# An attention stage with two MLPs behind it: the linear part of the first MLP formed as (h w_in)ᵀ scaled by alpha times w_out

## The chip, the cores and the metric

The kernel runs on one core of a Trainium2 chip. The metric is the device time of one execution in microseconds, the median of several runs. Lines are named by their number in the kernel before (L585 is line 585).

## The reference

12480 tokens of 128 channels go through an attention over 32 inducing points and then through two MLPs with a hidden width of 2048.

```
scale = 1/sqrt(128)
def mab(q, kv):                       # a softmax, then a @ kv
    s = scale * (q @ kv.T);  s -= s.max(-1)
    a = exp(s);  a /= a.sum(-1) + 1e-9
    return a @ kv
h  = mab(inducing, x)                 # first attention: 32 x 128
x1 = mab(x, h)                        # second attention: 12480 x 128
t  = x1 @ w_in                        # 12480 x 2048
y1 = (max(t, 0) + alpha * min(t, 0)) @ w_out
y2 = max(y1 @ w2_in, 0)**2 @ w2_out   # the output, float32
```

The kernel uses two identities. With a the softmax weights of the second attention, x1 = a h, so t = a (h w_in) and the 32 x 2048 matrix h w_in can be made once. And max(t,0) + alpha min(t,0) = (1 - alpha) max(t,0) + alpha t, so that y1 = relu(t) ((1 - alpha) w_out) + a V with the small matrix V = h w_in diag(alpha) w_out. V is the linear part.

## The kernel before

Inputs come as 64-bit floats and are converted on the chip, piece by piece (512 columns each, four pieces for each of the four weights). `to_f32` (L179) makes four steps of a piece: `magnitude` and `low`, one pass each on ScalarE (ACT); `bits` on VectorE (DVE); `sign`, which is one DVE instruction and an addition on GpSimd (POOL) that writes the float32 piece. `conv_w_out` (L212) adds three: `rest` (POOL) multiplies the piece by 1 - alpha into `aw`; `split` rounds that to `wo_hi` (ACT) and puts the remainder into `wo_lo` (POOL); `scaled` overwrites `aw` with alpha times w_out, in four ACT instructions. `convs[0..3]` are the pieces of w_in, `convs[4..7]` those of w_out.

The first attention runs over seven groups of tokens (L353 to L408): scores, maxima, exponentials, transposes and values, with a running maximum. One piece is converted beside each group, up to `convs[4]`. The tail (L387 to L426) combines the groups and gives `hT`, the transposed h (L420). Ahead of and behind `hT` stand four calls of `transpose_w_in` (L379): four TensorE transposes and an ACT copy each, which give `wiT`.

From L526 on the second attention of the first token tile (`first`) and of tiles 1 to 3 (`second`) is prepared, and h w_in is made in four pieces: `make_w1s(k)` on TensorE, `split_w1s(k, 0)` on ACT and `split_w1s(k, 1)` on DVE. `first[6]` and `first[7]` spread the softmax weights over the partitions and write `a_s`, which the first hidden matmul (L585) reads.

The main loop (L738) is written out by hand as steps s = 0, 1, ...: at each, `l1_a(s)` makes one 128-wide slice of the hidden layer (matmul L585, Relu on ACT L589, remainder on DVE L591); `l1_b` (three matmuls) follows 3 to 5 steps later, the second MLP 24 steps later. One tile of tokens takes 16 steps. A `plan` adds further work to steps: the pieces of w_out that are left, `make_w1s(2)` at s=2 and `make_w1s(3)` at s=5, `second[2]` to `second[6]` at s=0 to 7, and the pieces of the second MLP's weights at s=11, 13, 17 and later. V is made by `step_u` (s=16 to 19, 16 matmuls of `wiT` with `aw`), `copy_u` and `step_v` (s=20); it is wanted at s=22.

Every engine works through its instructions in the order in which they are written, and so does the queue of SyncE (SP) that issues the DMAs. `second[6]` (s=7) issues 12 DMAs there, the load of the third weight piece of the second MLP (w2_out piece 0, `at(9, load_w, ...)`) stands right behind them, and ACT's `magnitude` of that piece is planned at s=17. PSUM banks go round: h1 and h2 have two each, which odd and even l1_a share with `make_w1s(0)` and `(1)`.

Of the kernel before, what the change touches and what calls it, by code (L numbers as in the profile page):

```python
# [25 lines left out]
Q = 4  # L26
# [3 lines left out]
def attention_then_two_mlps(ctx: ExitStack, tc, x, inducing, w_in, w_out, alpha, w2_in, w2_out, out):  # L30
# [7 lines left out]
    P = 128  # L38
# [61 lines left out]
    ident = cv.tile([P, P], F32, name="ident", tag="u_sb", bufs=1)  # L100
    make_identity(nc, ident)

    same = st_tile("same", [P, P])
# [25 lines left out]
    wiT = keep.tile([P, DFF], F32, name="wiT", tag="w2o_hi")  # L129
# [49 lines left out]
    def to_f32(name, k, place):  # L179

        v = {}

        def magnitude():
            raw = raws.pop((name, k))
            v["h"], v["l"] = raw[:, :, 1], raw[:, :, 0]
            v["m"] = cv.tile([P, 512], F32, name="mag", tag="mag", bufs=3)
            nc.scalar.mul(v["m"], v["h"].bitcast(F32), 2.0**-112)  # L190
# [12 lines left out]

        return [magnitude, low, bits, sign]
# [7 lines left out]
    def conv_w_out(k):  # L212
        chunks, cols = slice(4 * k, 4 * k + 4), slice(k * 512, (k + 1) * 512)
        f, hi, lo, a = (v.rearrange("p c d -> p (c d)")[:, cols] for v in (w_out_sb, wo_hi, wo_lo, aw))

        def rest():
            nc.gpsimd.tensor_tensor(
                aw[:, chunks], w_out_sb[:, chunks], al1[:, chunks].unsqueeze(2).to_broadcast([P, 4, P]), op=ALU.mult
            )

        def scaled():
            for c in range(4 * k, 4 * k + 4):
                nc.scalar.activation(aw[:, c, :], w_out_sb[:, c, :], AF.Copy, scale=al[:, c : c + 1])

        def split():
            nc.scalar.copy(hi, a)
            pool_lo(lo, a, hi)


        return to_f32("w_out", k, lambda: f) + [rest, split, scaled]  # L230
# [122 lines left out]
    for g in range(last):  # L353
# [13 lines left out]
        if g:  # L367
            convs[g - 1][3]()
# [10 lines left out]
    def transpose_w_in(k):  # L379
        b = y2_bank()  # L380
        for i in range(4):
            c = 4 * k + i
            nc.tensor.transpose(b[:, i * P : (i + 1) * P], w_in_sb[:, c * P : (c + 1) * P], ident)
        nc.scalar.copy(wiT[:, k * 512 : (k + 1) * 512], b)
# [18 lines left out]
    nc.vector.tensor_scalar_mul(nnm, nm[last], -1.0)  # L403
    wgt = att.tile([P, 1], F32, name="wgt", tag="wgt")
# [4 lines left out]
    run(convs[5][:2])  # L409
# [7 lines left out]
    transpose_w_in(0)  # L417
# [6 lines left out]
    transpose_w_in(1)  # L424
    run(convs[5][2:4])
    convs[4][4]()  # L426
# [98 lines left out]

    first = second_attention([0], [0, P, 2 * P])  # L526
# [25 lines left out]


    u_bank = []

    def step_u(k):
        if k == 0:
            u_bank.append(y2_bank())
        for c in range(4 * k, 4 * k + 4):
            nc.tensor.matmul(  # L560
                u_bank[0][:, :P], wiT[:, c * P : (c + 1) * P], aw[:, c, :], start=(c == 0), stop=(c == NCH - 1)
            )

    u_sb = cv.tile([P, P], F32, name="u_sb", tag="u_sb", bufs=1)

    def copy_u():
        nc.scalar.copy(u_sb, u_bank[0][:, :P])

    def step_v():
# [95 lines left out]
    AW = [8, 7, 16, 15]  # L665
# [117 lines left out]
```

## Time and profile before

| | us |
|---|---|
| median of 3 runs | 975.65 (975.25 to 976.1) |
| the profiled execution, whole | 976.26 |
| its span, first to last instruction | 974.2 |
| TensorE busy (matmul) | 960.8 |
| ACT / DVE / POOL busy | 756.2 / 671.9 / 543.8 |

The busy shares are means over a front part of some 95 us and a long main loop with other limits, so they are read by stretch. A line of the timeline gives the start, the duration, the engine, the source line, the output and the input, and in brackets how long the engine had been idle and what ended that.

### The profile page before, as it was taken

What the parts mean: (1) busy time and instruction counts of PE and PEld (TensorE: products, weight loads), DVE (VectorE), ACT (ScalarE), POOL (GpSimd) and SP (SyncE); (2) the same over time, 40 slices, a digit from 0 to 9 for tenths busy, and PEclk for the clock granted to TensorE, in tenths of its full rate; (3) what the DMA queues carried; (4) which work ended last, traced back from release to release, by engine and by line L of the source; (5) the groups of instructions that cost most, each with busy time, mean ns of one, the idle gap of its engine ahead of it and who ended that gap; (6) DMA issues with size and microseconds to landing.
All of it is one profiled execution on the core that took longest, in us unless ns stands there. A gap on an engine that the chain in (4) does not pass through costs nothing.

```text
span 974.2 us, 15128 instructions
## 1 busy us (share of the span) xinstructions
PE 960.8 (99%) x5034; PEld 882.3 (91%) x5034; DVE 671.9 (69%) x1130; ACT 756.2 (78%) x1501; POOL 543.8 (56%) x484
## 2 busy tenths in 40 slices
PE   9899999999999999999999999999999999999998
PEld 7677999998999989999899999899998999999997
DVE  6789776666766667666677666676666766666677
ACT  5689877777777777777787777787777777777776
POOL 2368765555665556655556555566555665555530
PEclk9989999999999999999999999999999999999999
DMA  9432002000020000110000200002000010000001
GB/s 329 152 92 68 9 3 46 11 10 1 10 48 10 1 10 10 28 21 10 10 10 3 46 11 10 1 11 48 10 1 10 10 32 18 10 10 10 1 10 19
DMA packets 65933, 28.35 MB, mean 29 GB/s; under 512 B 53968, under 2 KB 61760, under 8 KB 65856
## 3 DMA queue, kind: packets, MB, share of 16 engines
q1 hardware_dynamic: 64928, 27.29, 11.2%
q8 instruction: 39, 0.64, 0.3%
q14 instruction: 38, 0.31, 0.1%
q10 hardware_dynamic: 928, 0.11, 0.1%
HBM read 14.80 MB, written 6.39 MB: 22 GB/s over the span
## 4 chain that ended last, share of the span: by engine, by line
PE 95%; DVE 2%; ACT 2%; issue 1%; DMA 0%; ACTq 0%; DVEq 0%
PE y L595 18%; PE y L597 18%; PE y L596 18%; PE h L595 9%; PE h L597 9%; PE h L596 9%; PE h L585 9%; PE h L267 1%; PE ms L281 1%; PE y L331 1%; PE y L613 1%; PE ms L444 1%; DVE g1l L591 0%; DMA raw<-in_moe_w_out_dram 0%; ACT g1h L589 0%
## 5 line engine op out<-in xcount | busy, mean ns | idle before, releaser
L640 POOL TENSOR_TENSOR g2l<-sq,g2h 128x448 fp32r<-128x448 f32 (+1 forms) x424 | 486.6, 1148 | 343.7 <-ACT g2h L638 336.3
L591 DVE SCALAR_TENSOR_TENSOR g1l<-h,g1h 128x448 fp32r<-128x448 f32 (+1 forms) x448 | 277.6, 620 | 225.8 <-ACT g1h L589 220.5
L589 ACT ACTIVATE g1h<-h 128x448 fp32r<-128x448 f32 (+1 forms) x448 | 243.9, 545 | 136.0 <-PE h L585 132.3
L631 DVE TENSOR_TENSOR sq<-h,r 128x448 f32<-128x448 f32 (+1 forms) x448 | 278.4, 621 | 48.9 <-ACT r L629 4.8
L629 ACT ACTIVATE r<-h 128x448 f32<-128x448 f32 (+1 forms) x448 | 244.4, 545 | 54.3 <-PE h L597 8.8
L638 ACT CAST g2h<-sq 128x448 fp32r<-128x448 f32 (+1 forms) x448 | 249.4, 557 | 1.8 <-DVE sq L631 1.7
L585 PE MATMUL h<-a_s,w1s 128*128 128x448 f32 (+1 forms) x448 | 165.5, 371 | 3.2 <-DVE g1l L591 1.7
L595 PE MATMUL h<-y1h,w2i_hi 128*128 128x448 f32 (+1 forms) x448 | 162.7, 363 | 0.1
L597 PE MATMUL y<-g1l,wo_hi 128*128 128x448 f32 (+1 forms) x448 | 162.5, 363 | 0.0
L596 PE MATMUL y<-g1h,wo_lo 128*128 128x448 f32 (+1 forms) x448 | 162.4, 363 | 0.0
L595 PE MATMUL y<-g1h,wo_hi 128*128 128x448 f32 (+1 forms) x448 | 162.4, 362 | 0.0
L597 PE MATMUL h<-y1l,w2i_hi 128*128 128x448 f32 (+1 forms) x448 | 162.1, 362 | 0.2 <-DVE y1l L617 0.2
L595 PE MATMUL y<-g2h,w2o_hi 128*128 128x448 f32 (+1 forms) x448 | 162.1, 362 | 0.0
L597 PE MATMUL y<-g2l,w2o_hi 128*128 128x448 f32 (+1 forms) x448 | 162.1, 362 | 0.0
L596 PE MATMUL y<-g2h,w2o_lo 128*128 128x448 f32 (+1 forms) x448 | 162.0, 362 | 0.0
L596 PE MATMUL h<-y1h,w2i_lo 128*128 128x448 f32 (+1 forms) x448 | 161.9, 361 | 0.0
L585 PEld LDWEIGHTS h<-a_s,w1s 128*128 128x128 f32 (+1 forms) x448 | 84.9, 190 | 16.6 <-DVE g1l L591 5.7
L595 PEld LDWEIGHTS h<-y1h,w2i_hi 128*128 128x128 f32 x448 | 84.1, 188 | 7.3 <-DVE sq L631 1.4
L595 PEld LDWEIGHTS y<-g1h,wo_hi 128*128 128x128 f32 x448 | 84.5, 189 | 5.6 <-issue 0.5
L597 PEld LDWEIGHTS h<-y1l,w2i_hi 128*128 128x128 f32 x448 | 84.1, 188 | 5.9 <-DVE y1l L617 0.5
L597 PEld LDWEIGHTS y<-g2l,w2o_hi 128*128 128x128 f32 x448 | 84.1, 188 | 5.7 <-DVE g2l L640 0.2
L596 PEld LDWEIGHTS y<-g1h,wo_lo 128*128 128x128 f32 x448 | 84.4, 188 | 5.3
(127 smaller groups left out, 727.0 us busy)
## 6 DMA issues: line engine op xcount, KB each, us to landing
out_dram<-o SPq DMA_DIRECT2D x106, 56.0 KB, 1.9
xg<-in_x_dram SPq DMA_DIRECT2D x10, 512.0 KB, 8.8
raw<-in_moe_w_in_dram SPq DMA_DIRECT2D x8, 512.0 KB, 5.5
raw<-in_moe_w_out_dram SPq DMA_DIRECT2D x8, 512.0 KB, 4.9
a_s<-a_hi SPq DMA_DIRECT2D x54, 56.0 KB, 2.0
a_s<-a_lo SPq DMA_DIRECT2D x54, 56.0 KB, 1.9
xg<-in_x_dram SPq DMA_DIRECT2D x4, 256.0 KB, 3.5
out_dram<-o SPq DMA_DIRECT2D x4, 48.0 KB, 1.8
```

What stands on the lines that cost most here:

```text
L267: nc.tensor.transpose(b[:, k * p : (k + 1) * p], x_t[g][:p, i, k, :], ident[:p, :p])
L281: nc.tensor.matmul(b[i * M : (i + 1) * M, :n], indT, xT[:, t0 : t0 + n], start=True, stop=True, tile_position=(0, i * M),)
L585: nc.tensor.matmul(b[:, :w], w1s[: a.shape[0], c * P : (c + 1) * P], a, start=True, stop=True)
L589: nc.scalar.activation(hi, b[:, :w], AF.Relu)
L591: nc.vector.scalar_tensor_tensor(lo, b[:, :w], 0.0, f32(hi), op0=ALU.max, op1=ALU.subtract)
L595: nc.tensor.matmul(b, w_hi, hi, start=start, stop=False)
L596: nc.tensor.matmul(b, w_lo, hi, start=False, stop=False)
L597: nc.tensor.matmul(b, w_hi, lo, start=False, stop=stop)
L629: nc.scalar.activation(r, b, AF.Relu)
L631: nc.vector.tensor_tensor(sq, b, r, op=ALU.mult)
L638: nc.scalar.copy(hi, sq)
L640: (nc.vector if i >= total - LAG2 else nc.gpsimd).tensor_tensor(lo, sq, f32(hi), op=ALU.subtract)
```

## The change

The transposes of w_in, the sixteen `scaled` activations and `step_u` go. `step_wa` makes (h w_in)ᵀ, chunk by chunk of 128 hidden rows, from `w_in_sb` as the stationary operand and 32 columns of `hT`: eight chunks behind `make_w1s(0)`, four at s=0, four at s=1. `scale_wa` multiplies all of it by alpha in one DVE instruction (s=2). `step_v` multiplies it with `w_out_sb` (16 matmuls in four column groups, s=10); `copy_v` and `split_v` sum the four groups by a matmul with `same` (s=11, 14).

The conversions of w_out move: `convs[4]`'s `rest` and high part, and steps of `convs[5]`, `[6]` and `[7]`, stand in the tail of the first attention; `sign` and its POOL addition are now separate steps, and so are the high and the low part. `make_w1s(1)` and its `split` move from ahead of the loop to s=0, `second[2]` from s=0 to 1, `second[4]` from 2 to 3, `second[5]` from 4 to 5.

```diff
-    same = st_tile("same", [P, P])
+    same = keep_tile("same", [P, P])
...
+        def add():
+            nc.gpsimd.tensor_tensor(place().bitcast(I32), v["c"], v["l"], op=ALU.add)
+        return [magnitude, low, bits, sign, add]
...
-        def scaled():
-            for c in range(4 * k, 4 * k + 4):
-                nc.scalar.activation(aw[:, c, :], w_out_sb[:, c, :], AF.Copy, scale=al[:, c : c + 1])
-        def split():
+        def high():
             nc.scalar.copy(hi, a)
+        def low():
             pool_lo(lo, a, hi)
...
+    MAG, LOW, BITS, SIGN, ADD, REST, HI, LO = range(8)
     b = scores(last)
     values1(last - 1)
+    convs[4][REST]()
+    convs[5][MAG]()
+    convs[6][MAG]()
     maxima(last, b)
     exps(last, b)
     b = y2_bank()
     nc.tensor.transpose(b[:1, :P], nm[last], ident)
+    convs[4][HI]()
     transpose_e(last)
...
     nc.vector.tensor_scalar_mul(nnm, nm[last], -1.0)
+    convs[5][BITS]()
+    convs[5][SIGN]()
+    convs[6][BITS]()
...
     values1(last)
-    run(convs[5][:2])
+    convs[5][LOW]()
+    convs[5][ADD]()
+    convs[6][LOW]()
+    run(convs[7][:2])
...
-    transpose_w_in(0)
...                                   # here hT is made
-    transpose_w_in(1)
-    run(convs[5][2:4])
-    convs[4][4]()
+    convs[4][LO]()
+    convs[7][BITS]()
...
     first[0]()
     make_w1s(0)
-    transpose_w_in(2)
-    run(convs[6][:2])
+    step_wa(range(8))
     run(first[1:4])
     split_w1s(0, 0)
+    stage1.close()
+    run(first[4:6])
+    split_w1s(0, 1)
+    convs[6][SIGN]()
+    convs[6][ADD]()
+    convs[5][REST]()
+    convs[5][HI]()
+    first[6]()
     second[0]()
-    transpose_w_in(3)
-    stage1.close()
-    make_w1s(1)
-    convs[5][4]()
-    run(first[4:6])
-    convs[4][5]()
-    split_w1s(0, 1)
-    first[6]()
-    convs[6][2]()
     first[7]()
-    convs[6][3]()
-    convs[6][4]()
+    convs[7][SIGN]()
+    convs[6][REST]()
+    convs[5][LO]()
     second[1]()
-    split_w1s(1, 0)
...
-    at(0, convs[5][5])
+    at(0, step_wa, range(8, 12))
+    at(0, make_w1s, 1)
+    at(0, split_w1s, 1, 0)
+    at(0, convs[6][HI])
     at(1, split_w1s, 1, 1)
-    at(0, second[2])
+    at(1, step_wa, range(12, 16))
+    at(1, convs[7][ADD])
+    at(1, convs[6][LO])
+    at(1, second[2])
+    at(2, scale_wa)
     at(2, make_w1s, 2)
     at(2, split_w1s, 2, 0)
     at(2, second[3])
-    at(2, second[4])
-    at(3, convs[6][5])
-    at(5, split_w1s, 2, 1)
-    at(4, second[5])
-    at(2, convs[7][0])
-    at(5, convs[7][1])
-    at(5, convs[7][2])
+    at(3, convs[7][REST])
+    at(3, second[4])
+    at(4, split_w1s, 2, 1)
+    at(5, second[5])
     at(5, make_w1s, 3)
     at(5, split_w1s, 3, 0)
+    at(5, convs[7][HI])
+    at(5, convs[7][LO])
     at(7, split_w1s, 3, 1)
     at(7, second[6])
-    at(7, convs[7][3])
-    at(8, convs[7][4])
-    at(13, convs[7][5])
-    for k in range(4):
-        at(AW[k], convs[4 + k][6])
-        at(16 + k, step_u, k)
-    at(19, copy_u)
-    at(20, step_v)
+    at(10, step_v)
+    at(11, copy_v)
+    at(14, split_v)
```

The new functions:

```
def step_wa(chunks):                  # one PSUM bank for all chunks
    for c in chunks:
        matmul(wa_bank[:, c*M:(c+1)*M], w_in_sb[:, c*P:(c+1)*P], hT[:, :M])
def scale_wa():
    nc.vector.tensor_tensor(wa, wa_bank, al, op=mult)    # alpha broadcast over 32
def step_v():
    for c in range(NCH):
        q = c % Q
        matmul(v_bank[q*M:(q+1)*M, :P], wa[:, c, :], w_out_sb[:, c, :], tile_position=(0, q*M))
def split_v():
    matmul(bv[:, :P], same, v_sb)     # then v_s as before, on ACT and DVE
```

## Rows read from the trace of the kernel before

**Rows 1.** Windows view: stretch, length, busy us (count) of PE, PEld, DVE, ACT, POOL; clock, DMA share, GB/s

```profile
47.70:58.20 10.50, 9.25 (x22) 6.28 (x23) 9.82 (x18) 7.24 (x16) 6.10 (x5) 0.54 0.00 0
58.20:71.20 13.00, 12.57 (x78) 11.51 (x77) 10.21 (x17) 12.37 (x34) 7.43 (x6) 1.00 0.45 121
...
95.00:950.00 855.00, 855.00 (x4297) 796.98 (x4290) 580.76 (x947) 669.03 (x1309) 497.39 (x436) 1.00 0.07 14
```

**Rows 2.** Timeline, 35 to 48 us: first attention's tail to the first hidden matmul

```profile
35.16 0.69 ACT L306 ACTIVATE e<-ms,nm 128x512 f32<-128x512 f32 x1 [1.89 <-DVE nm L299]
...
37.62 0.29 DVE L407 TENSOR_SCALAR sel<-same,wgt 128x128 f32<-128x128 f32 x1 [1.17 <-ACT wgt L405]
...
39.83 0.42 DVE L197 TENSOR_SCALAR mag<-mag 128x512 int32<-128x512 int32 x1
...
40.28 0.69 DVE L201 SCALAR_TENSOR_TENSOR mag<-raw,mag 128x512 int32<-128x512 int32 x1
...
40.89 0.30 DVE L452 STREAM_TRANSPOSE a<-y 96x128 f32<-96x128 f32 x1
...
41.55 1.00 DVE L458 TENSOR_TENSOR a<-a,mx 96x128 f32<-96x128 f32 x1
...
43.64 0.29 ACT L461 ACTIVATE a<-a 96x128 f32<-96x128 f32 x1
...
45.37 0.69 DVE L522 TENSOR_TENSOR w1s<-h,w1s 64x512 fp32r<-64x512 f32 x1
...
46.09 0.94 DVE L197 TENSOR_SCALAR mag<-mag 128x512 int32<-128x512 int32 x1
46.37 0.47 ACT L505 CAST a_s<-y 96x384 fp32r<-96x384 f32 x1 [0.96 <-PE y L498]
...
47.06 0.55 DVE L507 TENSOR_TENSOR a_s<-y,a_s 32x384 fp32r<-32x384 f32 x1
...
47.67 1.33 PE L585 MATMUL h<-a_s,w1s 96*128 96x384 f32 x3 [1.34 <-DVE a_s L507]
```

**Rows 3.** Timeline, 41 to 47 us: one piece's steps on POOL and ACT

```profile
41.11 1.29 POOL L202 TENSOR_TENSOR w_out_sb<-mag,raw 128x512 int32<-128x512 int32 x1 [6.38 <-ACT wiT L384]
...
42.35 2.09 POOL L217 TENSOR_TENSOR aw<-w_out_sb,al 128x512 f32<-128x512 f32 x2
...
44.78 0.62 ACT L226 CAST wo_hi<-aw 128x512 fp32r<-128x512 f32 x1
...
45.48 1.27 POOL L207 TENSOR_TENSOR wo_lo<-aw,wo_hi 128x512 fp32r<-128x512 f32 x1 [1.04 <-ACT wo_hi L226]
```

**Rows 4.** Timeline, 48 to 59 us: terms of the loop's first eight steps

```profile
48.79 1.91 PE L517 MATMUL y<-w_in_sb,hT 128*128 128x512 f32 x2
...
50.03 1.27 DVE L458 TENSOR_TENSOR a<-a,mx 96x448 f32<-96x448 f32 x1
...
52.99 0.60 DVE L466 TENSOR_REDUCE sm<-a 96x14 f32<-96x448 f32 x1
...
53.99 0.95 DVE L591 SCALAR_TENSOR_TENSOR g1l<-h,g1h 128x384 fp32r<-128x384 f32 x2
...
55.19 0.64 DVE L474 STREAM_TRANSPOSE a2t<-a 96x448 f32<-96x448 f32 x1 [0.24 <-POOL a L470]
...
58.17 0.56 ACT L483 CAST a_hi<-a2t 96x448 fp32r<-96x448 f32 x1
```

**Rows 5.** Timeline, 58 to 72 us: alpha's activations, the SP queue, the late load

```profile
58.63 1.28 ACT L223 ACTIVATE aw<-w_out_sb,al 128x128 f32<-128x128 f32 x4
...
59.98 0.51 SPq L489 DMA_DIRECT2D a_s<-a_lo  x1
...
65.24 1.03 PEld L560 LDWEIGHTS y<-aw,wiT 128*128 128x128 f32 x8
...
66.92 0.53 SPq L172 DMA_DIRECT2D raw<-in_moe_w_out_dram  x1
...
71.23 0.68 ACT L190 ACTIVATE mag<-raw 128x512 f32<-128x512 f32 x1 [0.66 <-DMA raw<-in_moe_w_out_dram]
```

More of the change, by code (lines that the diff above doesn't have):

```diff
@@ L128, in attention_then_two_mlps @@
     w_out_sb = keep.tile([P, NCH, P], F32, name="w_out_sb", tag="w2i_lo")
-    wiT = keep.tile([P, DFF], F32, name="wiT", tag="w2o_hi")
     aw = keep.tile([P, NCH, P], F32, name="aw", tag="w2o_lo")
@@ L219, in rest @@
             )
-        def scaled():
-            for c in range(4 * k, 4 * k + 4):
-                nc.scalar.activation(aw[:, c, :], w_out_sb[:, c, :], AF.Copy, scale=al[:, c : c + 1])
-        def split():
+        def high():
             nc.scalar.copy(hi, a)
+        def low():
             pool_lo(lo, a, hi)
-        return to_f32("w_out", k, lambda: f) + [rest, split, scaled]
+        return to_f32("w_out", k, lambda: f) + [rest, high, low]
     def conv_w2(name, k, hi, lo):
@@ L367, in attention_then_two_mlps @@
         if g:
-            convs[g - 1][3]()
+            run(convs[g - 1][3:5])
         if 1 < g and g + 3 <= last:
@@ L377, in attention_then_two_mlps @@
             nc.vector.tensor_scalar(al1, al, -1.0, 1.0, op0=ALU.mult, op1=ALU.add)
[L379 to L384, printed above, removed]
+    MAG, LOW, BITS, SIGN, ADD, REST, HI, LO = range(8)
     b = scores(last)
     values1(last - 1)
+    convs[4][REST]()
+    convs[5][MAG]()
+    convs[6][MAG]()
     maxima(last, b)
@@ L524, in split_w1s @@
             nc.scalar.copy(dst, b)
+    wa = att.tile([P, NCH, M], F32, name="wa", tag="wa")
+    wa_bank = []
+    def step_wa(chunks):
+        if not wa_bank:
+            wa_bank.append(y2_bank())
+        for c in chunks:
+            nc.tensor.matmul(
+                wa_bank[0][:, c * M : (c + 1) * M], w_in_sb[:, c * P : (c + 1) * P], hT[:, :M], start=True, stop=True
+            )
+    def scale_wa():
+        nc.vector.tensor_tensor(
+            wa, wa_bank[0].rearrange("p (c j) -> p c j", j=M), al.unsqueeze(2).to_broadcast([P, NCH, M]), op=ALU.mult
+        )
     first = second_attention([0], [0, P, 2 * P])
@@ L529, in attention_then_two_mlps, with step_v, copy_v @@
     make_w1s(0)
-    transpose_w_in(2)
-    run(convs[6][:2])
+    step_wa(range(8))
     run(first[1:4])
     split_w1s(0, 0)
-    second[0]()
-    transpose_w_in(3)
-    stage1.close()
-    make_w1s(1)
-    convs[5][4]()
-    run(first[4:6])
-    convs[4][5]()
-    split_w1s(0, 1)
-    first[6]()
-    convs[6][2]()
+    stage1.close()
[6 more added lines that the diff above has]
+    first[6]()
+    second[0]()
     first[7]()
-    convs[6][3]()
-    convs[6][4]()
+    convs[7][SIGN]()
+    convs[6][REST]()
+    convs[5][LO]()
     second[1]()
-    split_w1s(1, 0)
     load_w("w2_in", 0)
     load_w("w2_in", 1)
[L554 to L559, printed above, removed]
+    v_bank = []
+    def step_v():
+        v_bank.append(y2_bank())
+        for c in range(NCH):
+            q = c % Q
             nc.tensor.matmul(
-                u_bank[0][:, :P], wiT[:, c * P : (c + 1) * P], aw[:, c, :], start=(c == 0), stop=(c == NCH - 1)
-            )
[L564 to L569, printed above, removed]
+                v_bank[0][q * M : (q + 1) * M, :P], wa[:, c, :], w_out_sb[:, c, :],
+                start=(c < Q), stop=(c >= NCH - Q), tile_position=(0, q * M),
+            )
+    v_sb = cv.tile([P, P], F32, name="v_sb", tag="v_sb", bufs=1)
+    def copy_v():
+        nc.scalar.copy(v_sb, v_bank[0][:, :P])
+    def split_v():
         bv = free_bank()
-        nc.tensor.matmul(bv[:, :P], hT, u_sb, start=True, stop=True)
+        nc.tensor.matmul(bv[:, :P], same, v_sb, start=True, stop=True)
         nc.scalar.copy(v_s, bv[:, :P])
@@ L664, in attention_then_two_mlps @@
     LAG1, LAG1_EARLY, LAG2, LAG2B, EARLY = 3, 5, 24, 4, 20
-    AW = [8, 7, 16, 15]
     PIECES = [
```

6 lines of the change are left out of this document (2 added, 4 removed).

## The prediction

> **What bounds the kernel now.** I read the windows view first. From 95 to 950 us TensorE's matmuls cover 855.00 of 855.00 us at full clock, 4297 of them, 0.199 us each [rows 1]. Nothing that the change touches lies there, so the time of the whole follows the front part one to one: if the loop reaches its saturated stretch 1 us later, the kernel ends 1 us later. The question is only when that is. In the front part two stretches matter. From 47.7 to 58.2 us TensorE ran at a granted clock of 0.54, so nearly all the time at its lower level of 1.2 GHz, and DVE was busy 9.82 of 10.50 us. From 58.2 to 71.2 us the clock was full and ACT was busy 12.37 of 13.00 us [rows 1]; ACT is the engine that the change relieves, so the eye goes there.
>
> Then I read the timeline of that ACT stretch, and how it ends. The piece of w2_out that ACT opens at s=17 begins at 71.23 us, and what ended ACT's idle time ahead of it (0.66 us) is a DMA [rows 5]. That DMA is issued at 66.92 us, because it stands in SP's queue behind the 12 issues of `second[6]`: the second of these is at 59.98 us, and eleven steps of 0.63 us lead to 66.92; it lands 4.3 us later [rows 5]. The 12 issues in turn start when ACT writes `a_hi` at 58.17 us [rows 4]. So a fixed 13.06 us lies between `a_hi` (s=7) and the opening of that piece (s=17), however little ACT has to do in between. I call it the lid. What counts is when `a_hi` comes.
>
> Last I read the timeline of the tail of the first attention, from 35 us to the first hidden matmul L585 at 47.67 us [rows 2], for what each moved step stands ahead of.
>
> **The change part by part, the stretch of ACT's relief.** Sixteen alpha activations leave ACT, four groups of 1.28 us, 5.1 us [rows 5]. They all stood between `a_hi` and s=17. Without them, and with the last high part (0.62 us [rows 3]) gone to s=5, ACT would have 13.06 - 0.66 - 5.1 - 0.62 = 6.7 us to do there. DVE has ten remainders of 0.48 us [rows 4], one split of 0.69 and two pieces' bits and signs at 0.42 and 0.69 [rows 2], with POOL's blocks about 9 us. Both lie under the lid, so the relief is worth only the 0.66 us of slack that it makes larger: nothing at the end. The matmuls for V go the same way: 32 loads of 0.129 us [rows 5] for u leave s=16 to 19, 32 loads for `step_wa` come in, and `step_v` at s=10, which the trace does not show, costs between 0 and those 4.1 us; it lies under the lid too, so 0 at the end. Behind s=17 ACT loses the copy of u and that of v, and DVE the remainder of v. Each has 128 columns; at the rate of the 384-wide pair, 0.95 us for 768 [rows 4], two are 0.3 us. The bounds are 0 and 0.95; I take -0.3.
>
> **The front part up to hT.** The two `magnitude` passes put ahead of the last exponential fall into ACT's wait of 1.89 us for the maximum [rows 2]: two of about 0.69 are 1.4. `rest` of piece 4 is a POOL step of 1.05 us (half of 2.09 [rows 3]) while POOL is free. Its high part, 0.62 us, goes between the last exponential and the copy of its transposes; bits, sign and bits on DVE, 0.42 + 0.69 + 0.42 = 1.53 us, go into DVE's idle 1.17 us before `sel` [rows 2], and the 0.4 us that sticks out is covered by the values matmuls, which `sel`'s reader comes behind. Were that cover gone, `hT` would be 0.4 us later. I take 0.
>
> **From hT to the first hidden matmul.** Here one thing gains and one loses. ACT no longer has a copy of `wiT` and the two passes of `convs[6]` ahead of the exponential L461, which stood at 43.64 us although its input was ready at 42.55 (41.55 + 1.00) [rows 2]. The input itself: `convs[7]`'s bits stand on DVE ahead of the transposes L452, where those of `convs[5]` stood at 39.83. At that time POOL is busy with `wo_lo` of piece 4: the addition of piece 5 can start when ACT's low pass is done, 37.6 + 0.7 = 38.3, takes 1.29, and `wo_lo` follows for 1.27, to 40.85 [rows 3]. The trace shows what such a bits step costs beside POOL: at 46.09 it took 0.94 us instead of 0.42 and ended 0.28 us after POOL's `wo_lo` had (45.48 + 1.27 = 46.75) [rows 2, 3]. So it ends at 41.1 us, or at 40.25 if POOL doesn't hold it. I take the first, as the row is of the same two instructions. (The Trainium skill, page "SBUF — State Buffer", section "Who interferes with whom", says the same more generally: the two engines share one pair of ports, and whichever comes second waits for the whole instruction of the other. By that the term is the first of the two, and the sum below +1.7; otherwise it would be +1.15.) L452 then starts at 41.15, the subtraction 0.66 later as before; it took 1.00 under POOL's addition, and between 0.15 and that without, I take 0.30, as the transpose of the same shape. The exponential starts at 42.15 us: 1.5 us sooner than before.
>
> From the exponential's start to DVE's `split_w1s(0, 1)` it took 1.73 us (43.64 to 45.37), so that one is at 43.9. And now the new wait. ACT's high part of piece 5 is written ahead of the copy of `a_s` in `first[7]`. It reads what POOL's `rest` of piece 5 writes, POOL has the addition of piece 6 ahead of that, and this addition waits for DVE's sign of piece 6, which stands behind the split. In a row: split to 44.6 (0.72 to the next start), sign 0.69 to 45.3, addition 1.29 to 46.6, `rest` 1.05 to 47.7, high part 0.62 to 48.3 [rows 2, 3]. Behind it are queued, on ACT, the copy of `a_s` (0.47), on DVE its remainder (0.55), and on TensorE the first L585: 49.4 us [rows 2]. Without the high part in front the copy could go when the spread is done, about 3.3 us sooner. The first L585 is thus at 49.4 against 47.67, **+1.7 us**, and TensorE has nothing to do for some 3.6 us before it.
>
> **From the first hidden matmul to a_hi.** Before: 47.67 to 58.17, 10.5 us. After, L585 of s=1 no longer follows directly. TensorE first has eight loads of `step_wa` and `make_w1s(1)`. At full clock that is 8 x 0.129 and about 0.9 us; at the lower level 8 x 0.26 and 1.75 to 1.91 us [rows 4, 5]. Which level? Before, it was the lower one through this whole stretch [rows 1], though TensorE had idled only 1.34 us directly ahead of it [rows 2]. After a longer hole I take the lower. [...] So L585 of s=1 starts 0.35 + 2.1 + 1.75 = 4.2 us after the first. ACT then does a split and the high part of piece 6 (two starts, 1.1 us) before its Relu of s=1 (0.5): 5.8 us. From there DVE has in order: remainder 0.5, split 0.72, maximum 0.60 (as the sum), subtraction 0.6 to 1.27, remainder 0.5, `scale_wa` 0.72 (not in the trace; between the 0.30 of a small transpose and the 1.27 of that subtraction; 512 PSUM columns like the split), remainder 0.5, sum with reciprocal 1.0 (52.99 to 53.99), remainder 0.5, split 0.72, remainder 0.5, transposes 0.64 [rows 2, 4]: 7.5 us. POOL's product lies beside them. `a_hi` comes 13.3 us after the first L585: **+2.8 us**; with the full clock 11.3 us, +0.8.
>
> **The sum.** +1.7 + 2.8 = +4.5 for `a_hi`; the lid passes it on to s=17; -0.3 behind that: +4.2 us. It is made in the profiled execution, whose 976.26 us (span 974.2) stand 0.6 us over the median; a difference carries over. 975.65 + 4.2 = 979.85 us.
>
> **The rivals.** *The clock stays up, or POOL doesn't hold the bits.* At full clock the sum is 1.7 + 0.8 - 0.3 = +2.2, without the hold another 0.55 less: 977.3 to 977.9 us; the hold gone and the clock low: 979.3. For it: `step_wa`'s 16 loads behind `make_w1s(0)` keep TensorE busy some 2 us longer. Against it: the 3.6 us hole.
>
> *A second drop of the clock.* ACT would idle some 4 us under the lid, and TensorE runs out of free banks with it. If the clock falls there, about four steps of s=18 to 22 run four matmuls at 0.4 instead of 0.2 us, 1.6 us against about 1.2 of ACT: +1.5, 981.3 us. In this stretch before TensorE was busy 12.57 of 13.00 us and the clock was 1.00 [rows 1], so nothing shows it.
>
> *Not slower: the wait in front of `a_s` is hidden.* That needs the high part of piece 5 to be done when the spread ends, near 44.8 us, so DVE's sign of piece 6 to be done by 41.8 us, 3.5 us sooner than I have it. Then the first L585 comes at 46.0, the hole is short, the clock full: -1.7 + 0.8 - 0.3 = -1.2, 974.45 us.
>
> *The lid doesn't hold.* If that load came earlier (issues faster than 0.63 us apart, or landed in less than 4.3 us), ACT's relief would count: the stretch would be DVE's 9 us instead of 13.06, -4. With the low clock +0.2, 975.85 us; with the full clock -1.8, 973.85 us. Against it: twelve issues in a row held that pace.
>
> **How the numbers follow.** Forecast 0.42; clock up or no hold 0.20; second drop 0.12; wait hidden 0.12; no lid 0.14. A measurement of this kernel tells about 0.2% (1.95 us) from no change, so the limits are 973.7 and 977.6 us. Slower: 0.42 + 0.12 + 0.12 of the first rival = 0.66. Same: the other 0.08, 0.08 of the hidden wait, 0.06 of no lid = 0.22. Faster: 0.04 + 0.08 = 0.12. The range leaves out the hidden wait and the better end of no lid: 975.5 to 982.0 us; the forecast's own range is 978.7 to 980.8.
>
> **What would show it.** The exponential L461 near 42 us; the high part of piece 5 ending near 48.3 with the copy of `a_s` right behind it and idle on its engine put down to POOL; the first hidden matmul near 49.4; `a_hi` near 62.7 after a stretch at the lower clock; ACT's wait for the DMA of w2_out grown from 0.66 to about 4 us; then the same course as before, later. If the copy of `a_s` starts with the spread's end, or if ACT's wait at s=17 has not grown, the prediction is wrong in that step.

## The result, and the profile after

The changed kernel takes 986.27 us, the median of four runs (985.43 to 989.03), against 975.67 us (975.25 to 976.1) before: a ratio of 1.0114 [1.0093, 1.0135]. That is 10.6 us slower where 4.2 were forecast, and outside the range. The profiled execution took 989.03 us with a span of 986.3, so it stands 2.8 us over its median; the two spans differ by 12.1 us.

The start of some rows in both profiled executions gives the places. The columns are the two durations, their difference, and the difference that the prediction had. hT is the end of DVE's L420 (after: L421); the first hidden matmul is L585 (after: L599); g(18) is ACT's Relu of s=18, r(28) and r(471) are ACT's first passes of the second MLP for s=28 and for the last step.

| stretch | before | after | differs | predicted |
|---|---|---|---|---|
| start to hT | 39.91 | 41.10 | +1.19 | 0 |
| hT to the first hidden matmul | 7.76 | 9.29 | +1.53 | +1.7 |
| to a_hi | 10.50 | 13.52 | +3.02 | +2.8 |
| to g(18) | 13.64 | 13.48 | -0.16 | 0 |
| to r(28) | 14.63 | 15.81 | +1.18 | -0.3 |
| to r(471) | 879.87 | 885.24 | **+5.37** | 0 |

The first line is not put down to the change: in this execution TensorE waited 1.12 us, up to 7.96 us, for a transfer of x, and in the other profiled executions hT comes between 39.5 and 40.9 us, in kernels with the changed front (39.5 to 40.9) as in those with that of before (39.8 to 40.2). The next four sum to +5.57 us, the last alone to +5.37.

The page of the kernel after, its span and the busy time of each engine:

```profile
span 986.3 us, 15141 instructions
...
PE 968.7 (98%) x5050; PEld 884.7 (90%) x5050; DVE 672.2 (68%) x1131; ACT 749.6 (76%) x1481; POOL 544.5 (55%) x484
```

ACT lost 6.6 us of work against the table of before, as the change meant, and TensorE's busy time grew by 7.9. The windows view of the front part, cut at hT, the first hidden matmul, a_hi and s=17 (columns: stretch, length, then busy time and instructions of PE, PEld, DVE, ACT and POOL, TensorE's granted clock, DMA share, GB/s):

```profile
41.10:50.40 9.30, 6.01 (x37) 3.51 (x37) 5.15 (x13) 1.77 (x4) 4.85 (x5) 0.74 0.16 56
50.40:63.90 13.50, 13.02 (x45) 9.92 (x46) 9.54 (x18) 6.55 (x14) 6.26 (x6) 0.68 0.01 1
63.90:76.80 12.90, 11.62 (x86) 9.56 (x84) 9.98 (x18) 7.76 (x18) 4.36 (x5) 1.00 0.42 118
76.80:91.40 14.60, 12.17 (x44) 9.95 (x44) 12.11 (x20) 12.90 (x27) 7.92 (x7) 0.77 0.48 160
```

The second line answers to the stretch at 0.54 in [rows 1]: 13.50 us instead of 10.50. The granted clock was at its lower level, 1.2 GHz, from 45.5 to 59.2 us (before: 47.2 to 57.5), and again from 79.6 to 86.5 us, which is the 0.77 of the fourth line; before had no such second drop. (An early one, from 8.0 to 11.4 us, belongs to the first line of the table.) The timeline shows the wait ahead of the first hidden matmul, and the late load:

```profile
40.71 1.28 POOL L208 TENSOR_TENSOR wo_lo<-aw,wo_hi 128x512 fp32r<-128x512 f32 x1
41.01 1.26 DVE L196 TENSOR_SCALAR mag<-mag 128x512 int32<-128x512 int32 x1
...
43.16 0.31 ACT L461 ACTIVATE a<-a 96x128 f32<-96x128 f32 x1 [2.11 <-DVE a L458]
...
46.44 1.28 POOL L203 TENSOR_TENSOR w_out_sb<-mag,raw 128x512 int32<-128x512 int32 x1 [4.45 <-issue]
47.68 2.04 POOL L218 TENSOR_TENSOR aw<-w_out_sb,al 128x512 f32<-128x512 f32 x2
48.76 0.62 ACT L223 CAST wo_hi<-aw 128x512 fp32r<-128x512 f32 x1 [4.82 <-POOL aw L218]
49.28 0.47 ACT L505 CAST a_s<-y 96x384 fp32r<-96x384 f32 x1
49.78 0.55 DVE L507 TENSOR_TENSOR a_s<-y,a_s 32x384 fp32r<-32x384 f32 x1 [3.48 <-ACT a_s L505]
50.39 0.69 PE L599 MATMUL h<-a_s,w1s 96*128 96x384 f32 x1 [2.57 <-DVE a_s L507]
...
63.91 0.57 ACT L483 CAST a_hi<-a2t 96x448 fp32r<-96x448 f32 x1 [0.98 <-DVE a2t L474]
...
76.82 0.67 ACT L189 ACTIVATE mag<-raw 128x512 f32<-128x512 f32 x1 [2.79 <-DMA raw<-in_moe_w_out_dram]
```

ACT stands 4.82 us in front of the high part of piece 5, waiting for POOL, and the copy of `a_s`, its remainder and the first hidden matmul follow in a row, as the prediction has it. At the lower end ACT now waits 2.79 us for the DMA of w2_out ([rows 5]: 0.66).

The other half is in the stretch that [rows 1] shows as covered in full. The windows view of 300 to 800 us, same columns, first of before, then of after:

```profile
300.00:800.00 500.00, 500.00 (x2511) 465.25 (x2510) 338.86 (x552) 390.19 (x763) 291.16 (x255) 1.00 0.07 14
```

```profile
300.00:800.00 500.00, 500.00 (x2495) 462.92 (x2495) 337.38 (x549) 387.72 (x757) 288.45 (x253) 1.00 0.07 13
```

TensorE is busy 500.00 us of 500.00 at full clock in both, but it gets 2495 matmuls done instead of 2511: 0.64% fewer, 3.2 us in these 500. Which ones, the groups of the same stretch tell (columns: line, operation, tiles, shape, count, busy us, mean ns of one, idle). Before, all ten forms have a mean of 362 to 364 ns, for instance:

```profile
L597 PE MATMUL y<-g2l,w2o_hi 128*128 128x448 f32 x246 | 89.2, 362 | 0.0
L596 PE MATMUL y<-g2h,w2o_lo 128*128 128x448 f32 x246 | 89.2, 362 | 0.0
```

After:

```profile
L610 PE MATMUL y<-g2h,w2o_lo 128*128 128x448 f32 x245 | 89.9, 367 | 0.0
L611 PE MATMUL y<-g1l,wo_hi 128*128 128x448 f32 x245 | 89.8, 367 | 0.0
L611 PE MATMUL y<-g2l,w2o_hi 128*128 128x448 f32 x245 | 89.6, 366 | 0.0
L609 PE MATMUL y<-g2h,w2o_hi 128*128 128x448 f32 x245 | 89.6, 366 | 0.0
...
L609 PE MATMUL y<-g1h,wo_hi 128*128 128x448 f32 x244 | 88.4, 362 | 0.0
L610 PE MATMUL h<-y1h,w2i_lo 128*128 128x448 f32 x244 | 88.4, 362 | 0.0
```

Four of the ten are longer by 3 to 5 ns: the three that use w2_out's halves and the one just ahead of them (consecutive matmuls overlap, so that a duration is longer than the pitch; from start to start it is 203.2 instead of 200.0 ns at these four places). These are the four pairs of neighbours of which one at least reads `w2o_hi`. Four times 3.2 ns in each of the 425 steps from s=46 to 471 is 5.4 us; the starts of the ACT passes put 5.3 us on them. The instructions there are the same in both kernels. What differs is where `w2o_hi` lies: in the program's allocation of SBUF it starts at byte 107424 of a partition before, in the place that it shares by its tag with `wiT`, and at 117440 after, since the change removes `wiT` and the tile is then made last. Each of the six other large weight tiles of the loop (`w1s`, `wo_hi`, `wo_lo`, `w2i_hi`, `w2i_lo`, `w2o_lo`) starts at a byte whose rest modulo 512 is 416 in both kernels (that of the small `v_s` is 32 in both); that of `w2o_hi` was 416 and is 192.

### The profile page after: what moved, and what is told of

It reads as the page before. It is cut to its first block, busy times and chain, and to the rows that moved or that the text cites. A ratio compares the mean times of both kernels' runs of the same rounds, so it can differ in the third digit from the quotient of the medians.

```text
span 986.3 us, 15141 instructions
## 1 busy us (share of the span) xinstructions
PE 968.7 (98%) x5050; PEld 884.7 (90%) x5050; DVE 672.2 (68%) x1131; ACT 749.6 (76%) x1481; POOL 544.5 (55%) x484
## 4 chain that ended last, share of the span: by engine, by line
PE 93%; DMA 2%; DVE 1%; ACT 1%; SPq 1%; issue 1%; POOL 0%; ACTq 0%; DVEq 0%
PE y L611 18%; PE y L610 18%; PE y L609 18%; PE h L609 9%; PE h L611 9%; PE h L610 9%; PE h L599 9%; DMA raw<-in_moe_w_in_dram 1%; DMA xg<-in_x_dram 1%; SPq L489 1%; PE y L627 1%; PE ms L444 1%; DMA raw<-in_moe_w_out_dram 0%; PE h L265 0%; PE ms L279 0%
## 5 line engine op out<-in xcount | busy, mean ns | idle before, releaser
L599 PE MATMUL h<-a_s,w1s 128*128 128x448 f32 (+1 forms) x448 | 167.2, 374 | 6.5 <-DVE g1l L605 3.2
L599 PEld LDWEIGHTS h<-a_s,w1s 128*128 128x128 f32 (+1 forms) x448 | 85.7, 191 | 22.9 <-DVE g1l L605 6.5
L610 PEld LDWEIGHTS y<-g2h,w2o_lo 128*128 128x128 f32 x448 | 84.6, 189 | 6.7
L611 PEld LDWEIGHTS y<-g1l,wo_hi 128*128 128x128 f32 x448 | 84.5, 189 | 5.5
```

Source lines behind the costliest of these rows:

```text
L599: nc.tensor.matmul(b[:, :w], w1s[: a.shape[0], c * P : (c + 1) * P], a, start=True, stop=True)
L610: nc.tensor.matmul(b, w_lo, hi, start=False, stop=False)
L611: nc.tensor.matmul(b, w_hi, lo, start=False, stop=stop)
```

## The experiments

Four theories: the address of `w2o_hi` costs 5 us in the loop; the high part of piece 5 ahead of the copy of `a_s` costs 3 to 4; the late load (the lid) and the second drop cost 1 to 2 together; and, as a rival to the first, something else that the change does slows the long loop (more traffic, another order). The median of before was 976.44 us beside e1 to e4, 976.77 beside e5 and e7 to e9, and 976.02 beside e6, e10 and e11. Since it moves by 1.1 us from 975.67 to the highest of these, each kernel is told by its difference from the before beside it, as after is by its 10.6 us; what one difference is less than another is called a gain.

**The changed kernel with `w2o_hi` where it was.** In e1 the tile is made at the point where `wiT` was, and starts at 107936 (rest 416):

```diff
+    w2o_first = keep.tile([P, DFF], F32R, name="w2o_hi", tag="w2o_hi")
     aw = keep.tile([P, NCH, P], F32, name="aw", tag="w2o_lo")
...
-            w2.extend(keep.tile([P, DFF], F32R, name=v, tag=v) for v in ("w2o_hi", "w2o_lo"))
+            w2.extend([w2o_first, keep.tile([P, DFF], F32R, name="w2o_lo", tag="w2o_lo")])
```

> The changed kernel with one tile moved: the rounded half of the second MLP's output weights, w2o_hi, is allocated where wiT stood in the kernel before (between w_out_sb and aw), and not at the end of its pool. No instruction changes. Theory 1 (the address of w2o_hi costs 3.2 ns in each of the matmul steps that touch it): in the long loop the matmuls on g2h and g2l start 200 ns apart as in the kernel before, where the changed kernel has 203; over 448 steps of four such gaps that is 5.3 us, so about 981 us. Rival (the gap comes from something that the change does to the loop's order, or from the chip's state in those runs): 203 ns stay, about 986 us.

Measured: 981.58 us (980.62 to 983.16), 1.0049 [1.0033, 1.0065], 5.1 us over before, a gain of 5.5 from after. The same stretch of its windows view, columns as above:

```profile
300.00:800.00 500.00, 500.00 (x2510) 465.24 (x2510) 338.48 (x551) 390.45 (x762) 290.19 (x254) 1.00 0.07 13
```

2510 matmuls again, and from s=28 on the kernel stands 6.24 to 6.28 us behind before at nearly every step: it no longer falls back. The rival falls: the changed order and traffic are all still there, and the loop is as quick as before.

**The kernel before with only that tile moved.** In e2 nothing is changed but the line that makes `wiT`, so that tile and `w2o_hi` come to lie at 116928 (rest 192):

```diff
-    wiT = keep.tile([P, DFF], F32, name="wiT", tag="w2o_hi")
...
     indT = keep_tile("indT", [P, M])
+    wiT = keep.tile([P, DFF], F32, name="wiT", tag="w2o_hi")
```

> The kernel before with wiT, and with it w2o_hi, which takes its place later, allocated at the end of the same pool, as the changed kernel has it; no instruction changes. Theory 1 (address): the gaps of the matmuls on g2h and g2l go from 200 to 203 ns and the time from 975.7 to about 981 us, with the front part as it was. Rival (not the address): 975.7 us.

Measured: 982.09 us (981.73 to 983.26), 1.0057 [1.004, 1.0073], so 5.7 us for a line that computes nothing else.

```profile
300.00:800.00 500.00, 500.00 (x2495) 463.04 (x2495) 336.00 (x548) 387.47 (x758) 289.26 (x253) 1.00 0.07 13
```

2495 matmuls, as in after. Its front part is that of before to 0.3 us up to s=46, and then it falls back by 0.0125 us a step, to 5.5 us at the last one. In e1 against after and in e2 against before, `w2o_hi` is the only tile of the loop whose rest modulo 512 differs.

**The place or the address?** In e10 the changed kernel keeps its order, and `w2o_hi` stays the last tile; 224 unused bytes ahead of it put it at 117664, whose rest is 416 again:

```diff
+            keep.tile([P, 56], F32, name="pad0", tag="pad0")
             w2.extend(keep.tile([P, DFF], F32R, name=v, tag=v) for v in ("w2o_hi", "w2o_lo"))
+            keep.tile([P, 8], F32, name="pad1", tag="pad1")
```

> The changed kernel with w2o_hi left at the end of its pool, but 224 unused bytes ahead of it, so that its address leaves the rest 416 on division by 512, as those of the other five large weights do, where the changed kernel has 192 (32 more bytes behind it keep the tiles after it at multiples of 256 from where they were). Theory (the start of a weight tile within 512 bytes, not where in memory it lies, makes the 203 ns): the gaps go back to 200 ns and the time to about 981 us. Rival (the region, or the order of the tiles): 203 ns and 986 us.

Measured: 980.62 us (980.2 to 981.67), 1.0048 [1.0035, 1.0061], 4.6 us over before, a gain of 6.0 from after.

```profile
300.00:800.00 500.00, 500.00 (x2511) 465.40 (x2510) 338.16 (x551) 390.44 (x762) 291.40 (x255) 1.00 0.07 13
```

So it is the low bits of the address, not the region and not the order of the tiles. (No more than the rest modulo 512 is needed: modulo 2048 the tile has the rest 928 in before and in e10 and 1440 in e1, and its neighbours in e10 have 1440; the pitch is 200.0 ns in all three. 416 and 192 differ modulo 256 too, so the modulus may be smaller.)

**Other addresses.** In e9 the kernel before gets small pads, so that the rests modulo 512 are 416 for `w1s`, 448 and 480 for `wo_hi` and `wo_lo`, 0 and 32 for `w2i_hi` and `w2i_lo`, 64 and 128 for `w2o_hi` and `w2o_lo`, and 288 instead of 32 for `v_s`:

```diff
     w1s = keep_tile("w1s", [P, DFF], F32R)
+    pad0 = keep_tile("pad0", [P, 8])
     wo_hi = keep_tile("wo_hi", [P, NCH, P], F32R)
+    pad1 = keep_tile("pad1", [P, 8])
     wo_lo = keep_tile("wo_lo", [P, NCH, P], F32R)
...
```

> The kernel before with small unused tiles between the weights, so that their addresses leave these rests on division by 512: w1s 416 as before, wo_hi 448, wo_lo 480, w2i_hi 0, w2i_lo 32, w2o_hi 64, w2o_lo 128, v_s 288. Nothing else changes. Theory (the start of a weight tile within 512 bytes decides): the gaps of the three matmul groups differ from 200 ns where a rest is a costly one; w1s stays at 200. If only 416 is free, about 9 of 10 gaps take 203 ns, some 13 us more in the whole. Rival (it is not the start within 512 bytes but where in memory w2o_hi lay): 200 ns nearly everywhere, as in the kernel before.

Measured, in one execution: 983.36 us, 6.6 us over before; from s=28 on it falls 8.1 us behind. Its windows row and four of its groups, views and columns as above:

```profile
300.00:800.00 500.00, 500.00 (x2488) 461.37 (x2487) 335.17 (x547) 386.67 (x756) 288.86 (x252) 1.00 0.07 13
```

```profile
L602 PE MATMUL y<-g1h,wo_hi 128*128 128x448 f32 x244 | 90.2, 370 | 0.0
L603 PE MATMUL y<-g1h,wo_lo 128*128 128x448 f32 x244 | 89.6, 367 | 0.0
...
L592 PE MATMUL h<-a_s,w1s 128*128 128x448 f32 x244 | 88.3, 362 | 0.0
L602 PE MATMUL y<-g2h,w2o_hi 128*128 128x448 f32 x244 | 88.0, 361 | 0.0
```

The pitch now runs from 198 ns (`w2o_hi` to `w2o_lo`, and `w1s` to `w2i_hi`) to 207 ns (`wo_hi` to `wo_lo`), and around `v_s`, where before had 203.5 and 205 ns, one side came down to 200. So both neighbours matter, and some pairs are quicker than two equal rests. "Only 416 is free, all else costs 3 ns" is too simple, and no rule came out of this; that an all-round better set of addresses exists was not tried.

**The copy of `a_s` first.** e3 is the changed kernel with the high part of piece 5 behind it:

```diff
-    convs[5][HI]()
     first[6]()
     second[0]()
     first[7]()
+    convs[5][HI]()
```

> The changed kernel with one ACT instruction moved: the high part of w_out's piece 5 stands behind the copy of a_s in first[7] instead of ahead of it. Theory (the wait of ACT on POOL ahead of the copy delays the first hidden matmul by some 4 us and opens the hole in which TensorE's clock falls): the first hidden matmul comes 3.5 to 4 us sooner, about 6 us behind hT, and a_hi 4 to 5 us sooner; as the late load hangs on a_hi, the kernel ends 4 to 6 us sooner, 980 to 982 us. Rival (the length of DVE's own list between the first hidden matmul and a_hi sets a_hi anyway): a_hi moves by less than 1.5 us, 985 us or more.

Measured: 983.13 us (981.03 to 986.69), 1.0067 [1.0041, 1.0093], 6.7 us over before, a gain of 3.9 from after. Its timeline:

```profile
44.78 1.26 PE L498 MATMUL y<-a2t,same_q 96*128 96x128 f32 x6 [0.68 <-DVE a2t L474]
45.98 1.72 PE L444 MATMUL ms<-xT,hT 128*32 128x448 f32 x6
46.09 0.47 ACT L505 CAST a_s<-y 96x384 fp32r<-96x384 f32 x1 [2.37 <-PE y L498]
...
47.62 0.69 PE L599 MATMUL h<-a_s,w1s 96*128 96x384 f32 x1
...
61.15 0.57 ACT L483 CAST a_hi<-a2t 96x448 fp32r<-96x448 f32 x1
```

The first hidden matmul comes 6.8 us behind hT instead of 9.3. That is 2.5 us less (3.5 to 4 were expected), where the copy itself gained 3.0, because TensorE is next late: six score matmuls at half clock (1.72 us) are in front of it. a_hi gains the same 2.5 us (4 to 5 were expected). And the hole in TensorE's work is gone (the last idle time ahead is 0.68 us), yet the clock still fell, from 45.2 to 58.8 us, and the stretch to a_hi is 13.53 us, as in after (13.52). In after, too, the fall at 45.5 us came ahead of the hole, which lasts from 47.8 to 50.4. So the hole is not what made the clock fall. Another 1.46 us of gain in this profile lies between g(18) and r(28), where the second drop lasted 3.4 us instead of 6.8; over the four executions the mean granted clock goes from 0.985 (986.69 us) to 0.998 (981.03 us). So not all of the 3.9 us belongs to the moved instruction.

**Wide instead of narrow matmuls.** `step_wa` streams 32 columns through each loaded chunk. e8 is e3 with 128 columns streamed (what is written beyond a chunk's own 32 is overwritten by the next chunk):

```diff
+            w = min(P, NCH * M - c * M)
             nc.tensor.matmul(
-                wa_bank[0][:, c * M : (c + 1) * M], w_in_sb[:, c * P : (c + 1) * P], hT[:, :M], start=True, stop=True
+                wa_bank[0][:, c * M : c * M + w], w_in_sb[:, c * P : (c + 1) * P], hT[:, :w], start=True, stop=True
             )
```

> The changed kernel with the high part of piece 5 behind the copy of a_s, and step_wa streaming up to 128 columns of hT per weight load instead of 32 (the columns hold the same values four times; what a chunk writes beyond its own 32 columns the next chunk overwrites). Each pass then streams about as long as its weights take to load. Theory (TensorE's clock falls because in these microseconds the engine streams few columns, not because of the hole before the first hidden matmul): the fall, which came 4.3 us behind hT also without the hole, comes later or not at all, and a_hi 1.5 to 2.5 us sooner than in the run with the copy first: 980 to 981.5 us. Rival (the gaps count, however wide the matmuls are): the clock falls at the same place, and the time is that of the run with the copy first, 983 us.

Measured: 982.62 us (981.27 to 983.88), 1.0059 [1.0039, 1.0079], 5.9 us over before, a gain of 0.8 from e3, which the intervals do not tell from none: a_hi comes 2.1 us sooner, as expected, but the 980 to 981.5 us did not come. Windows of the first steps, of e3 and then of e8 (the clock is the third number from the end):

```profile
45.00:50.00 5.00, 5.00 (x22) 3.32 (x22) 3.13 (x5) 1.48 (x3) 3.78 (x4) 0.52 0.00 0
50.00:55.00 5.00, 5.00 (x15) 3.45 (x14) 2.21 (x4) 1.98 (x4) 4.47 (x4) 0.50 0.00 0
55.00:60.00 5.00, 5.00 (x15) 3.63 (x15) 4.59 (x10) 2.96 (x7) 1.15 (x2) 0.62 0.01 3
```

```profile
45.00:50.00 5.00, 4.73 (x34) 3.33 (x33) 3.55 (x5) 2.23 (x5) 4.39 (x4) 1.00 0.00 0
50.00:55.00 5.00, 3.11 (x13) 1.74 (x12) 4.09 (x7) 3.15 (x8) 4.43 (x4) 1.00 0.01 3
55.00:60.00 5.00, 4.83 (x29) 3.66 (x32) 4.84 (x11) 3.66 (x9) 3.06 (x3) 1.00 0.00 0
...
74.60:81.40 6.80, 6.19 (x17) 4.76 (x17) 6.10 (x9) 5.36 (x12) 4.70 (x4) 0.50 0.33 90
```

At full clock the first hidden matmul to a_hi takes 11.46 us (the prediction's full-clock value was 11.3). e10 is the closest partner: in both the clock fell at 40.4 us, and both then run the two 512-column matmuls of `make_w1s(0)` and the sixteen of `step_wa`. These rows are of e8, then of e10:

```profile
42.71 2.49 PE L534 MATMUL y<-hT,w_in_sb 128*128 128x128 f32 x16
```

```profile
42.63 3.46 PE L533 MATMUL y<-hT,w_in_sb 128*128 128x32 f32 x16
```

In e8 the clock came back at 43.8 us, during the wide ones; in e10 it stayed low to 60.9. That is one execution of each, and a third speaks against the width: e5 (below) has the narrow matmuls and the order of e3, and in its profiled execution the clock fell only at 53.3 us:

```profile
40.00:48.00 8.00, 7.06 (x50) 4.94 (x44) 6.76 (x14) 1.38 (x4) 3.54 (x4) 1.00 0.26 70
48.00:58.80 10.80, 8.11 (x29) 5.69 (x28) 8.76 (x17) 7.14 (x16) 8.11 (x7) 0.74 0.14 47
```

So where the clock falls differs from execution to execution with the same instructions, and that the width moves it is not shown. The gain of 2.1 us at a_hi in e8 was given back: with the lid still on, ACT waits 2.94 us for its load, the clock is low for 6.8 us instead of 3.4, and from g(18) to r(28) it takes 15.9 us instead of 14.35.

**The lid.** In e4 the changed kernel's load of w2_out goes ahead of the twelve issues of `second[6]`:

```diff
+    at(6, load_w, *PIECES[2][1:])
     at(7, split_w1s, 3, 1)
...
-    at(9, load_w, *PIECES[2][1:])
```

> The changed kernel with one DMA moved: the load of w2_out piece 0 is planned at s=6, ahead of the 12 DMAs of second[6] in SP's queue, instead of at s=9 behind them. Theory (the lid: that load sets when ACT opens the piece at s=17, and TensorE's clock falls in the wait): ACT's wait of 2.8 us for it is gone, the second stretch at the lower clock (6.8 us) too; 2.8 to 4.5 us sooner, 982 to 983.5 us. Rival (the pieces of the second MLP's weights that follow, or DVE, hold the loop to the same pace): less than 1 us sooner.

Measured: 984.67 us (983.55 to 985.94), 1.0079 [1.0064, 1.0094], 8.2 us over before, a gain of 2.4 from after. Timeline:

```profile
71.97 0.62 ACT L239 CAST w2i_hi<-wf 128x512 fp32r<-128x512 f32 x1 [1.14 <-POOL wf L203]
72.50 0.66 ACT L189 ACTIVATE mag<-raw 128x512 f32<-128x512 f32 x1
```

The wait for the DMA is gone, and a_hi to g(18) takes 10.66 us instead of 13.48. From there to r(28) it takes 0.8 us longer, and the clock still falls, from 80.5 to 83.9 us, though ACT no longer waits for the load: a shorter second drop than in after, where none was expected. So the lid was real and ACT's relief was worth nothing under it, and lifting it brought less in this execution (2.1 us up to r(28)) than the wait that it removed. The same two lines in the kernel before are e6:

> The kernel before with the load of w2_out piece 0 planned at s=6, ahead of the 12 DMAs of second[6], and nothing else changed. Theory (in the kernel before ACT is nearly as late as that load, so the late load costs it only the 0.66 us that ACT waits): -0.3 to -0.9 us, 975.9 to 976.4 against 976.8. Rival (the load is the bound there too, and what follows gains with it): 2 us or more sooner, 974.8 us or less.

975.54 us (974.34 to 977.17), 0.9996 [0.9987, 1.0005]: 0.5 us under before, as the theory had it, but not told from no difference; its profile shows 0.8 us less between a_hi and g(18). There ACT's own work fills the stretch, as the 0.66 us of [rows 5] says. With the load early in both, that stretch takes 12.85 us in the kernel before and 10.66 in the changed one: so ACT's relief is worth some 2 us there, as far as one execution of each tells.

**All three together.** e5 is after with the edits of e1, e3 and e4.

> The changed kernel with the three edits of the runs before together: w2o_hi where wiT stood, the high part of piece 5 behind the copy of a_s, the load of w2_out piece 0 ahead of the 12 DMAs. Theory (three separate costs: 4.7 us of address, 3.1 us of the wait, 1.6 us of the late load by the medians so far): they add up, 986.3 - 9.4 = 977 us, level with the kernel before (976.4). With the load no longer in the way the shorter front should count for more than that: 975 us is possible. Rival (the wait and the late load hide behind each other): 979 us or more.

975.31 us (973.49 to 977.3), 0.9984 [0.9972, 0.9995]. That is 1.5 us under before. The three single gains from after, 5.5 + 3.9 + 2.4 = 11.8 us of 10.6, would give 1.2 under it: by the medians they add up, within the 2 us or so to which each gain is known. In e5's profiled execution, at 977.3 us the slowest of its ten, hT to r(28) takes 47.6 us against 52.1 in after: 4.5 us less, where e3 and e4 alone show 3.8 and 2.1. So part of the two may hide behind each other when the clock falls. The loss is accounted for to within that, and of what the change could gain some 1.5 us remain.

**Less in the loop.** e7 is e5 with `make_w1s(1)`, its high part and all of `step_wa` ahead of the loop, in places where TensorE waits:

```diff
     stage1.close()
+    make_w1s(1)
     run(first[4:6])
...
     second[0]()
+    step_wa(range(8, 16))
     first[7]()
+    split_w1s(1, 0)
...
-    at(0, step_wa, range(8, 12))
-    at(0, make_w1s, 1)
-    at(0, split_w1s, 1, 0)
...
-    at(1, step_wa, range(12, 16))
```

> The run with all three edits, and besides make_w1s(1) with its high part ahead of the loop again as in the kernel before, and the last eight chunks of step_wa ahead of the loop too, behind the scores of second[0], so that nothing of them stands between the first two hidden matmuls. Theory (eight loads and make_w1s(1) at the lower clock hold the second hidden matmul 3.1 us back and with it DVE's list up to a_hi): from the first hidden matmul to a_hi it takes about 11 us instead of 13.5, and ACT's relief behind a_hi then counts: 972 to 974 us, sooner than both kernels. Rival (DVE's list between the two is as long without it): as the run with all three, within 1 us.

975.47 us (974.35 to 981.32), 0.9993 [0.9977, 1.0009]. A miss: the stretch to a_hi came down to 11.11 us as expected, but the first hidden matmul came 1.5 us later than in e5, and a_hi stands 18.57 us behind hT, in e5 18.61. The work was moved, not hidden.

**The three and the wide matmuls.** e11 is e5 with the edit of e8.

> The run with all three edits, and step_wa streaming up to 128 columns per weight load as in the wide run. Theory (the wide loads keep TensorE's clock up through the loop's first steps, and with the late load out of the way nothing takes the gain back): from the first hidden matmul to a_hi about 11.4 us instead of 12.7, 973 to 974.3 us, sooner than the kernel before. Rival (the pieces of the second MLP's weights and DVE hold the loop to the pace that it has anyway): 975 to 975.5 us as the run with all three.

975.84 us (973.65 to 978.27), 0.9993 [0.9982, 1.0003]. Another miss in the median. Its profiled execution, at 973.65 the fastest of its runs, kept the full clock through the whole front:

```profile
48.00:58.30 10.30, 7.44 (x35) 5.13 (x34) 8.61 (x17) 7.01 (x17) 7.83 (x7) 1.00 0.12 42
58.30:90.00 31.70, 28.84 (x168) 24.26 (x168) 29.66 (x48) 28.22 (x62) 20.59 (x17) 1.00 0.36 105
```

Still a_hi comes 18.22 us behind hT, in before 18.26. TensorE has gaps now (7.44 of 10.30 us); the chain through DVE and POOL to a_hi is next late, with DVE busy 8.61. The runs of this kernel lie 4.6 us apart, and the mean granted clock goes with them: 1.00 in three of the twelve (973.65 to 974.49 us), 0.995 to 0.998 in the other nine (974.94 to 978.27). e5, with the narrow matmuls, has 1.00 in three of its ten too (973.49 to 974.90 us); before has at most 0.998 in all of its executions beside these two. So what the change can gain comes mostly when the clock stays up: the middle ones of these three stand 1.9 us (e11) and 2.7 us (e5) under the median of before. This was read off afterwards, and what keeps the clock up stays open. No version was measurably quicker than e5, which is 0.16% under before.

## Why the prediction was wrong, step by step

*"Nothing that the change touches lies there, so the time of the whole follows the front part one to one."* This is the step that failed. I read [rows 1] as a stretch that cannot change because the same 4297 matmuls run in it. The change removes `wiT`, and with it the place of `w2o_hi`; the matmuls stay the same, and four of ten take 3.2 ns longer. The traces put 5.3 us (s=46 on) to 5.4 (s=28 on) on it, the medians of e1, e2 and e10 5.5 to 6.0. The line that makes `wiT`, and that the change takes out, has the tag `w2o_hi` in it (it stands in e2's edit); the trace of before had its hint too, since the fifteen matmuls with `v_s` in 300 to 800 us, whose rest is 32, stand 205 and 203.5 ns from their neighbours and all others of their shape 200.

*"A second drop of the clock"* was a rival at 0.12, with +1.5 us and the words "nothing shows it". It came: low from 79.6 to 86.5 us, and the stretch to r(28) is +1.18 where -0.3 was forecast, 1.48 off. The order of events is the one described: ACT waits for the load, TensorE idles 2.17 us behind it, up to 78.62, and 1.0 us later the clock falls. What sets the length of the drop is not shown: it lasts 6.8 us in after and e1 and 3.4 in e10, which differs from e1 by addresses alone. The evidence against it, TensorE's 12.57 of 13.00 us in [rows 1], was of a kernel in which ACT was not idle there; it should have had no weight. With this rival the effects on the front come to +5.7 us in the prediction's terms, and the changed kernel with its address restored stands 5.1 (e1) and 4.6 us (e10) over before.

*hT to the first hidden matmul, +1.7:* measured +1.53. DVE's bits took 1.26 us beside POOL's `wo_lo` and ended 0.28 us after it, as the row of the same two instructions had it. (The Trainium skill, page "SBUF — State Buffer", section "Who interferes with whom", has the later of the two engines wait for the whole instruction of the other when both want the ports that they share; the trace agrees, with 1.26 against 0.42 us alone.) The exponential came 2.06 us behind hT's end instead of some 3.7, the high part 5 ended at 49.4 with the copy of `a_s` behind it, and the idle time was put down to POOL.

*The first hidden matmul to a_hi, +2.8:* measured +3.02, at the lower clock as taken. The reason given for the level, the 3.6 us hole, was not the cause: the hole was 2.57 us and began 2.3 us after the fall, and e3 has no hole and the same stretch. That the level was right is in part luck, since in e5, with the order of e3, the clock stayed up to 53.3 us and the stretch took 12.65 us. (The Trainium skill, page "TensorE: Matmul & The Clock Gate", section "HAM oscillation — how this bites in real kernels", lays the loss of the full clock in one kernel to its waits between matmuls. In e3 the longest idle time of TensorE between hT and the fall is 0.68 us, so the trace shows no long wait there.)

*The lid, 13.06 us from a_hi to s=17:* it held, 12.91 us in after (63.91 to 76.82), and ACT's wait for the load grew to 2.79 us (about 4 was said). e4 shows that it hid ACT's relief.

*-0.3 behind s=17:* drowned in the second drop in after; in e3 and e10, where the drop lasted 3.4 us, g(18) to r(28) takes 14.35 and 14.37 us, 0.3 less than before. Not tested by itself.

Of the loss, then: some 5.5 us are the address, some 3.9 the wait in front of `a_s` with what the clock did in those runs, some 2.4 the lid, and against them stand some 1.5 us of gain that the other three hide. The address is known best, as the traces show it step by step; the runs of one kernel spread by 1.5 to 7 us, so the other sizes are good to about 2 us.

## What to carry to other kernels

An edit that removes or moves a tile moves others: compare the addresses of all tiles that the hot loop reads, and when a saturated stretch comes out longer, compare the count of instructions per time and the mean durations by form there before looking for waits. A conversion step put ahead of the instruction that opens the main loop, on the same engine, costs its whole chain if another engine feeds it; the chain has to be followed back to its first engine before the step is placed. Relief of an engine under a fixed transfer gains nothing and can lose, since what idles there may idle TensorE into its lower clock. And a difference of 1 or 2 us in a front part is put down to an edit only after the granted clock of all executions has been compared: here it differed between executions of one kernel.

## What was not expected of the hardware

The pitch of a matmul with 448 columns, each with its own weights of 128x128, depends on the addresses of the weight tiles: 200.0 ns with all seven at a rest of 416 modulo 512, 203.2 around one at 192, and 198 to 207 ns with rests mixed in e9. No run showed why. And a TensorE that is busy throughout can stay at 1.2 GHz: in e3 it did so from 45.2 to 58.8 us, with sixteen matmuls of 32 columns ahead and sixteen more in between. With 128 columns in their place (e8) the clock was full from 43.8 us on, but with the same narrow ones it was so from 40 to 53.3 us in e5: one front gave different clocks in different executions, and no run showed what decides.
